# Moving the transposes of the next group by one step, and the exponentials of the taps by two, in a fused dynamic-convolution and gated-MLP kernel

## The chip, the cores and the metric

The kernel runs on one core of a Trainium2 chip. The metric is the device time of one execution in microseconds (us). The kernel before takes 1408.44 us, the median of 3 runs (1408.35 to 1408.87).

## The reference

Two parts follow each other. A dynamic convolution: for each of 4 x 4096 tokens and 8 heads, 7 tap weights go through a softmax and weigh the 7 last tokens. Then a gated MLP on the 16384 tokens, 192 wide inside and out, 1536 in the middle, all in float32:

```python
w = weight_gen - np.max(weight_gen, axis=-1, keepdims=True)
w = np.exp(w)
w = w / (np.sum(w, axis=-1, keepdims=True) + 1e-09)
out = np.einsum('bshk,bskhg->bshg', w, x_unf)
...
g = x @ w_gate
silu = g * (1.0 / (1.0 + np.exp(-g)))
val = x @ w_val
return (silu * val @ w_out).astype(np.float32)
```

## The kernel before, in words

**Tiling.** Each of 128 partitions holds 128 tokens. Tokens are taken in `NG` = 32 groups of 4 columns (`JG`), that is 512 tokens a group; the middle width of 1536 is taken in `NF` = 12 slices of 128. The program is a list of 384 steps (g, f), and step i is written out by the loop at L618. Values that need float32 precision are split in two float32r halves, hi and lo, so most products are three matmuls. Matmuls use 64 rows of the array at a time: one for `LOW` and one for `HIGH`, which run side by side.

**One step (g, f).** `up_first` (L432) makes 12 matmuls into two PSUM tiles `up` (gate and value); `up_second` (L445) makes the last 6. ScalarE (ACT) takes silu of the first tile into `sg` (L459); VectorE (DVE) multiplies `h` = value x `sg` (L473), ACT rounds it to `hi` (L474), DVE makes `lo` (L476). Two steps later (`LAG` = 2) `down` (L483, L503 and L512) multiplies them with `w_out` into four accumulators, in two pairs, each in two halves: four calls a step. In an ordinary step three of them stand between `up_first` and `up_second`, and one behind.

**The pool of PSUM tiles.** `ps_up` has 4 tiles in turn. A step takes 2; in a turn step the transposes take the other 2 (`tr`).

**The attention of the next group.** While group g is multiplied, DVE makes `xatt` of group g+1: 13 operations (7 products L230, 6 additions L260) that `spread` (L546) lays over the steps from f = 9 of group g-1 (`LEAD` = 3) to f = 5 of group g. After the last addition ACT copies the upper columns of `xatt` to their place (L263). Then comes the **turn step**, from the table `turned`: in steady groups f = 6. There 8 transposes (`turn`, L295, instructions at L299) stand behind `up_first`, `up_second` follows at once, all four calls of `down` come behind it, then 8 more transposes; then `split_ops` (L312) makes `xhi` (ACT, L317) and `xlo` (DVE, L324) for group g+1, which begins 5 steps later. An order between the two halves of a sum is kept by a marker on GpSimd's queue (`told`, L278: wait for one matmul; `behind`, L284: the other half waits for the marker).

**The softmax of the taps.** Taps come in 6 chunks of 12, 24, 24, 24, 24 and 20 columns (3 groups, then 6 groups each, 5 in the last). For each chunk c >= 2, between steps s0 and s1 (72 steps): 4 DVE operations before (max L169, subtract L176, in two pieces), one exponential on ACT (L182) at step `at`, 5/8 of the way, and behind it sums, reciprocals and normalisation on DVE (L187 to L199). Exp and silu use different function tables, so ACT loads a table before the exponential (L182) and one before the next silu (L459). `at` is step 66, 138, 210 and 282: f = 6 in groups 5, 11, 17 and 23, which is a turn step. Chunk 1 has a place of its own, `EXP1` = 16: group 1, f = 4.

**Start.** In group 0 the weights are still being converted by DVE, ACT and GpSimd (`weight_ops`), and the turn step is step 8 (`LEAD1` = 1).

Of the kernel before, what the change touches and what calls it, by code (L numbers as in the profile page):

```python
# [18 lines left out]
def dynconv_glu_kernel(  # L19
# [35 lines left out]
    NF = F // P  # L55
# [4 lines left out]
    EXP1 = 16  # L60
# [59 lines left out]
    def load_taps(c):  # L120

        j0, n = wcuts[c]
        wt = w_t[c] = soft.tile([P, NJ, H, K], F32, tag="wt", name="wt")
        pieces = {0: (0, JG, n), 1: range(0, n + 1, 2 * JG)}.get(c, (0, n))

        def load(a, b):
            nc.sync.dma_start(
                out=wt[:, a:b].rearrange("p t h k -> p t (h k)"), in_=wgr[:, j0 + a : j0 + b]
            )

        return [lambda a=a, b=b: load(a, b) for a, b in zip(pieces, pieces[1:])]

    def load_x(c):

        j0, n = xcuts[c]
        xt = x_t[c] = xin.tile([P, PAD + NX, D], F32, tag="xt", name="xt")
        pieces = {0: (0, JG, n), 1: range(0, n + 1, 2)}.get(c, (0, n))

        def load(a, b):
            own = PAD if c and a == 0 else 0  # L140
            nc.sync.dma_start(
                out=xt[:, PAD + a - own : PAD + b], in_=xr[:, j0 + a - own : j0 + b]
            )
            if c == 0 and a == 0:


                per = S // T
                for p0 in range(0, P, per):
                    nc.gpsimd.memset(xt[p0 : p0 + 1, 0:PAD], 0.0)
                    nc.sync.dma_start(  # L150
                        out=xt[p0 + 1 : p0 + per, 0:PAD],
                        in_=xr[p0 : p0 + per - 1, T - PAD : T],
                    )

        return [lambda a=a, b=b: load(a, b) for a, b in zip(pieces, pieces[1:])]
# [156 lines left out]
    def split_ops(g, ps):  # L312
        hi = [xts.tile([P, NC], F32R, tag=f"xhi{half}", name="xhi") for half in range(2)]

        def high(half):
            def go():
                nc.scalar.activation(out=hi[half], in_=ps[half], func=AF.Copy)  # L317

            return go

        def low(half):
            def go():
                lo = xts.tile([P, NC], F32R, tag=f"xlo{half}", name="xlo")
                nc.vector.tensor_tensor(  # L324
                    out=lo, in0=ps[half], in1=hi[half].bitcast(F32), op=ALU.subtract
                )
                xT[g, half] = hi[half], lo

            return go

        return [high(0), low(0), high(1), low(1)]
# [5 lines left out]
    def load_weights(f):  # L337
        raw = stage.tile([P, NW, 2], I32, tag="raw", name="raw", bufs=RAW)
        fs = slice(f * P, (f + 1) * P)
        pieces = (  # L340
            (raw[:, 0:P], w_gate[0:P, fs]),
            (raw[:, P : 2 * P], w_val[0:P, fs]),
            (raw[0:DB, 2 * P : 3 * P], w_gate[P:D, fs]),
            (raw[DB:P, 2 * P : 3 * P], w_val[P:D, fs]),
            (raw[:, 3 * P : NW], w_out[fs]),
        )
        for dst, src in pieces:
            nc.sync.dma_start(out=dst.rearrange("p n w -> p (n w)"), in_=src.bitcast(I32))
        raw_t[f] = raw
# [194 lines left out]
    turned = {}  # L544

    def spread(ops, first, last):  # L546

        for n, op in enumerate(ops):
            at = first + (n * (last - first)) // len(ops)
            todo.setdefault(max(at, 0), []).append(op)  # L550

    with tc.manual_schedule():
        nc.gpsimd.memset(exp_bias, -920.0 * TWO23)

        nc.scalar.activation(out=warm, in_=exp_bias, func=AF.Exp)
        now, soon = load_x(0)
        for op in load_taps(0) + [now]:
            op()
        load_weights(0)
        load_weights(1)  # L560
        soon()
        for f in range(2, RAW):
            load_weights(f)
        make_identity(nc, ident)

        before, exponentials, after = softmax_ops(0)
        for op in before:
            op()
        convert = [weight_ops(f) for f in range(NF)]
        w0, w1, w2, w3 = convert[:4]  # L570
        nc.scalar.activation(out=warm, in_=exp_bias, func=AF.Silu)
        asides, rest, joined = attention_ops(0)
        for op in after[:3] + asides + rest[:4] + w0[:1] + [joined] + rest[4:5]:
            op()
        for op in [w0[1], rest[5], w0[2], w1[0], w0[3]] + rest[6:]:
            op()
        turns = split_ops(0, turn_whole(0))
        for op in turns[0::2] + w1[1:4] + turns[1:2] + w2[:1] + turns[3:]:
            op()

        later = after[3:]
        loads = load_x(1) + load_taps(1)
        todo[0] = [w2[1], w3[0], w2[2]]
        for i in range(NF):
            ops = todo.setdefault(i, [])
            for f, part in ((i + 2, 3), (i + 3, 1), (i + 4, 0), (i + 3, 2)):
                if f < NF:
                    ops.append(convert[f][part])
        todo[0] += later[:3]
        spread(loads, LOAD1, LOAD1 + 7)  # L590
        spread(later[3:], NF - LEAD - 2, NF - LEAD)
        spread(
            [lambda f=f: split(wo[:, f, 0], wo[:, f, 1], wo32[:, f]) for f in range(NF)],
            WO,
            NF + LAG - 1,
        )
        for c in range(1, len(wcuts)):
            s0 = (wcuts[c - 1][0] // JG - 1) * NF - LEAD if c > 1 else NF
            s1 = (wcuts[c][0] // JG - 1) * NF - LEAD
            before, exponentials, after = softmax_ops(c)  # L600
            at = s0 + (s1 - s0) * 5 // 8 if c > 1 else EXP1
            if c + 1 < len(wcuts):
                todo.setdefault(s1, []).append(lambda c=c: load_taps(c + 1)[0]())
            spread(before, s0 + 1 - (c == 1), at)
            exps[at] = exponentials
            spread(after, at + 2, s1)
        for g in range(1, NG):
            s0 = (g - 1) * NF - (LEAD if g > 1 else LEAD1)
            c = first_x.get(g)
            if c and c + 1 < len(xcuts):  # L610
                todo.setdefault(s0, []).append(lambda c=c: load_x(c + 1)[0]())
            asides, rest, _ = attention_ops(g)
            spread(asides, max(s0, 0), s0 + NF - 4)
            spread(rest, max(s0, 0), s0 + NF - 3)
            turned[s0 + NF - 3] = g

        steps = [(g, f) for g in range(NG) for f in range(NF)]
        for i in range(len(steps) + LAG + 1):  # L618
            ops = todo.pop(i, [])
            to_turn = turned.get(i)  # L620
            if i < len(steps):
                g, f = steps[i]
                sums, nop = up_first(g, f)
                if i in exps:
                    exps[i]()
            late = []
            if i > LAG:
                late = [(*steps[i - LAG - 1], 1, True)]
            if i > LAG and not to_turn:
                down(*late.pop())  # L630
            if to_turn:
                ps = [ps_up.tile([P, NC], F32, tag="up", name="tr") for _ in range(2)]
                turned_nop = turn(to_turn, ps, None)
            if LAG <= i < len(steps) + LAG:
                s = steps[i - LAG]
                late += [(*s, 0, False), (*s, 1, False), (*s, 0, True)]
                if not to_turn:
                    down(*late.pop(0))
                    if s[1]:
                        down(*late.pop(0))  # L640
                    else:
                        late.reverse()
            if i < len(steps):
                up_second(g, f, sums, nop)
                sg = silu(sums)
            for what in late:
                down(*what)
            if i > LAG:
                h_t.pop(steps[i - LAG - 1])
            if to_turn:  # L650
                turn(to_turn, ps, turned_nop)
            if i < len(steps):

                def between():
                    if ops:
                        ops.pop(0)()
                    return ops

                gated(g, f, sums, sg, between)
            if to_turn:  # L660
                for op in split_ops(to_turn, ps):
                    op()
            for op in ops:
                op()
# [33 lines left out]
```

## Time and profile before

| what | value |
|---|---|
| median of 3 runs | 1408.44 us |
| the profiled execution, its own time | 1409.2 us |
| its span, first to last instruction | 1407.4 us |
| PE (TensorE matmul) busy | 1300.9 us, 92% |
| PEld (TensorE weight load) busy | 1220.4 us, 87% |
| DVE (VectorE) busy | 1010.4 us, 72% |
| ACT (ScalarE) busy | 610.2 us, 43% |
| POOL (GpSimd) busy | 71.8 us, 5% |
| granted TensorE clock, mean | 0.988 |
| chain that ended last | PE 83%, DVE 8%, ACT 4%, DMA 2% |

Busy time is the union of an engine's instructions. PE counts matmuls whose ends are modelled, and LOW and HIGH matmuls overlap, so an instruction's length is more than the spacing of two. A row of the timeline gives start and length in us; "[0.76 <-X]" is idle time of that engine just before, and what ended it. A wait for several semaphores is put down to the one that the profile saw last. PEclk is the share of full clock that was granted to TensorE.

### The profile page before, as it was taken

How to read it: one execution, taken by the hardware profiler on the slowest of the kernel's cores; microseconds unless marked ns; L12 is line 12 of the kernel's file. 1: busy time of each engine (PE TensorE's matmuls, PEld its weight loads, DVE VectorE, ACT ScalarE, POOL GpSimd, SP SyncE). 2: the span in 40 equal slices, each digit the busy share in tenths (PEclk: the TensorE clock that was granted, in tenths of full speed). 3: DMA queues.
4: the chain of work that ended last, by engine and by line, in shares of the span. 5: the costliest groups of instructions: out<-in, count | busy, mean ns of one | idle time of the engine just before them, and what ended most of it. 6: DMA issues, size and time to landing. Idle time of an engine off the chain costs nothing.

```text
span 1407.4 us, 31625 instructions
## 1 busy us (share of the span) xinstructions
PE 1300.9 (92%) x13560; PEld 1220.4 (87%) x13560; DVE 1010.4 (72%) x1385; ACT 610.2 (43%) x1073; POOL 71.8 (5%) x66
## 2 busy tenths in 40 slices
PE   0479999999999999999999999999999999999998
PEld 0359899989999998999999899989989899999998
DVE  2997867768777777877777777777777776677743
ACT  1445444454444445444344544444454444444443
POOL 3673000000000000000000000000000000000000
PEclk9989999999999999999999999999999999999999
DMA  3341010101001010100101001010100101000000
GB/s 96 97 156 32 13 41 13 52 13 51 13 21 52 13 52 12 51 13 21 52 13 52 13 22 43 18 51 13 52 13 13 41 13 52 13 13 13 13 13 13
DMA packets 28460, 47.36 MB, mean 34 GB/s; under 512 B 1956, under 2 KB 25508, under 8 KB 26528
## 3 DMA queue, kind: packets, MB, share of 16 engines
q1 hardware_dynamic: 28320, 45.34, 9.7%
q8 instruction: 106, 1.74, 0.5%
q14 instruction: 34, 0.28, 0.1%
HBM read 32.75 MB, written 12.58 MB: 32 GB/s over the span
## 4 chain that ended last, share of the span: by engine, by line
PE 83%; DVE 8%; ACT 4%; DMA 2%; issue 1%; SPq 0%; ACTq 0%; DVEq 0%
PE dn L503 22%; PE up L451 19%; PE up L439 18%; PE up L442 17%; PE dn L512 6%; DVE xatt L260 3%; DVE h L473 2%; DMA xt<-in_x_dram 2%; ACT sg L459 2%; PE tr L299 1%; ACT xatt L263 1%; DVE m L389 1%; DVE w L402 1%; DVE m L379 0%; PE dn L496 0%
## 5 line engine op out<-in xcount | busy, mean ns | idle before, releaser
L503 PE MATMUL dn<-wo,hi 64*128 64x384 f32 x2976 | 612.7, 347 | 0.4 <-ACT hi L474 0.4
L512 PE MATMUL dn<-wo,lo 64*128 64x192 f32 x2976 | 543.0, 249 | 0.3 <-DVE lo L476 0.3
L503 PEld LDWEIGHTS dn<-wo,hi 64*128 64x128 f32 x2976 | 480.0, 185 | 14.9 <-ACT hi L474 0.6
L473 DVE TENSOR_TENSOR h<-up,sg 128x512 f32<-128x512 f32 x372 | 257.1, 691 | 289.5 <-ACT sg L459 289.4
L512 PEld LDWEIGHTS dn<-wo,lo 64*128 64x128 f32 x2976 | 444.8, 187 | 9.6 <-DVE lo L476 0.5
L459 ACT ACTIVATE sg<-up 128x512 f32<-128x512 f32 x384 | 229.7, 598 | 435.7 <-PE up L451 405.0
L474 ACT ACTIVATE hi<-h 128x512 fp32r<-128x512 f32 x372 | 235.2, 632 | 294.7 <-DVE h L473 294.7
L476 DVE TENSOR_TENSOR lo<-h,hi 128x512 fp32r<-128x512 f32 x372 | 255.8, 688 | 70.5 <-ACT hi L474 70.5
L439 PE MATMUL up<-xhi,wb_hi 64*128 64x512 f32 x768 | 246.8, 425 | 10.8 <-ACT sg L459 7.5
L451 PE MATMUL up<-xhi,wa_hi 64*128 64x512 f32 x768 | 240.4, 427 | 9.8 <-POOLq L280 9.7
L439 PE MATMUL up<-xlo,wb_hi 64*128 64x512 f32 x768 | 234.0, 395 | 0.9 <-DVE xlo L324 0.9
L439 PE MATMUL up<-xhi,wb_lo 64*128 64x512 f32 x768 | 234.0, 396 | 0.0
L442 PE MATMUL up<-xhi,wa_lo 64*128 64x512 f32 x768 | 233.0, 393 | 0.0
L442 PE MATMUL up<-xhi,wa_hi 64*128 64x512 f32 x768 | 233.0, 393 | 0.0
L442 PE MATMUL up<-xlo,wa_hi 64*128 64x512 f32 x768 | 231.8, 390 | 0.0
L451 PE MATMUL up<-xhi,wa_lo 64*128 64x512 f32 x768 | 226.1, 392 | 0.0
L451 PE MATMUL up<-xlo,wa_hi 64*128 64x512 f32 x768 | 225.6, 391 | 0.0
L230 DVE TENSOR_TENSOR prod<-xt,wt 128x768 f32<-128x768 f32 x186 | 182.0, 979 | 0.1
L260 DVE TENSOR_TENSOR xatt<-xatt,prod 128x768 f32<-128x768 f32 x186 | 180.7, 971 | 0.0
L439 PEld LDWEIGHTS up<-xhi,wb_hi 64*128 64x128 f32 x768 | 138.3, 186 | 16.4 <-ACT sg L459 8.3
L442 PEld LDWEIGHTS up<-xlo,wa_hi 64*128 64x128 f32 x768 | 138.9, 187 | 8.1
L442 PEld LDWEIGHTS up<-xhi,wa_lo 64*128 64x128 f32 x768 | 138.1, 185 | 8.8
(57 smaller groups left out, 1370.3 us busy)
## 6 DMA issues: line engine op xcount, KB each, us to landing
xt<-in_x_dram SPq DMA_DIRECT2D x14, 1344.0 KB, 5.6
out_dram<-osb SPq DMA_DIRECT2D x31, 384.0 KB, 2.6
raw<-in_moe_w_out_dram SPq DMA_DIRECT2D x12, 192.0 KB, 2.7
wt<-in_weight_gen_dram SPq DMA_DIRECT2D x3, 672.0 KB, 3.9
raw<-in_moe_w_gate_dram SPq DMA_DIRECT2D x12, 128.0 KB, 2.6
raw<-in_moe_w_val_dram SPq DMA_DIRECT2D x12, 128.0 KB, 2.6
wt<-in_weight_gen_dram SPq DMA_DIRECT2D x4, 224.0 KB, 3.7
xt<-in_x_dram SPq DMA_DIRECT2D x2, 384.0 KB, 3.7
```

Of the source, the lines that this page charges most:

```text
L230: engine.tensor_tensor(out=into.rearrange("p t (h i) -> p t h i", h=H), in0=src, in1=w, op=ALU.mult)
L260: nc.vector.tensor_tensor(out=a, in0=a, in1=tmp.pop(k), op=ALU.add)
L263: nc.scalar.activation(out=a[:, :, D:], in_=a[:, :, P:D], func=AF.Copy)
L439: nc.tensor.matmul(ps, w[r, fs], m[r], start=(n == 0), stop=False)
L442: ins = nc.tensor.matmul(sums[i], w[r, i, fs], m[r], start=False, stop=False)
L451: ins = nc.tensor.matmul(sums[i], w[r, i, fs], m[r], start=False, stop=(n == len(full) - 1))
L459: nc.scalar.activation(out=sg, in_=sums[0], func=AF.Silu)
L473: nc.vector.tensor_tensor(out=h, in0=sums[1], in1=sg, op=ALU.mult)
L474: nc.scalar.activation(out=hi, in_=h, func=AF.Copy)
L476: nc.vector.tensor_tensor(out=lo, in0=h, in1=hi.bitcast(F32), op=ALU.subtract)
L503: nc.tensor.matmul(acc[t], hi[r, cs], wo[r, f].rearrange("p a d -> p (a d)"), start=opens, stop=False,)
L512: nc.tensor.matmul(acc[t][:, 0:D], lo[r, cs], wo[r, f, 0], start=False, stop=closes)
```

## The change

Two numbers in the schedule. `at` becomes 2 steps earlier for chunks 2 to 5 (steps 64, 136, 208, 280: f = 4), and with it the DVE operations that are spread before and behind it move by 0 to 2 steps. `turned` becomes one step later for every group (f = 7; in group 0 step 9).

```diff
-            at = s0 + (s1 - s0) * 5 // 8 if c > 1 else EXP1
+            at = s0 + (s1 - s0) * 5 // 8 - 2 if c > 1 else EXP1
             if c + 1 < len(wcuts):
                 todo.setdefault(s1, []).append(lambda c=c: load_taps(c + 1)[0]())
             spread(before, s0 + 1 - (c == 1), at)
             exps[at] = exponentials
             spread(after, at + 2, s1)
...
             spread(rest, max(s0, 0), s0 + NF - 3)
-            turned[s0 + NF - 3] = g
+            turned[s0 + NF - 2] = g
```

TensorE's queue in group 1, the step f = 6, before (`dn_...` are accumulators; order gives the output's shape). The transposes stand directly behind `up_first`:

```order
L442 MATMUL up<-xhi,wa_lo 128x512 x2
L299 MATMUL tr<-ident,xatt 128x64 x8
L451 MATMUL up<-xhi,wa_hi 128x512 x2
L451 MATMUL up<-xlo,wa_hi 128x512 x2
L451 MATMUL up<-xhi,wa_lo 128x512 x2
L503 MATMUL dn_1064<-wo,hi 128x384
```

The same queue with the change, the end of `up_first` of f = 7 and what follows:

```order
L442 MATMUL up<-xhi,wa_lo 128x512 x2
L299 MATMUL tr<-ident,xatt 128x64 x8
L451 MATMUL up<-xhi,wa_hi 128x512 x2
L451 MATMUL up<-xlo,wa_hi 128x512 x2
L451 MATMUL up<-xhi,wa_lo 128x512 x2
L503 MATMUL dn_1065<-wo,hi 128x384
```

The neighbours are the same; one whole step of f = 6 in its ordinary order, with three calls of `down` ahead of `up_second`, now stands ahead of them.

ScalarE's queue in group 5, before: the exponentials stand behind the copy of `xatt` (L263) and ahead of the silu of the turn step, whose split (L317) follows.

```order
L459 ACTIVATE sg<-up 128x512
L474 ACTIVATE hi<-h 128x512
L263 ACTIVATE xatt<-xatt 128x4x64
L182 ACT_TABLE_LOAD
L182 ACTIVATE wt<-wt 128x1344
L459 ACT_TABLE_LOAD
L459 ACTIVATE sg<-up 128x512
L474 ACTIVATE hi<-h 128x512
L317 ACTIVATE xhi<-tr 128x512 x2
```

With the change they stand two steps ahead of the copy, and three ahead of the turn step's silu:

```order
L182 ACT_TABLE_LOAD
L182 ACTIVATE wt<-wt 128x1344
L459 ACT_TABLE_LOAD
L459 ACTIVATE sg<-up 128x512
L474 ACTIVATE hi<-h 128x512
L459 ACTIVATE sg<-up 128x512
L474 ACTIVATE hi<-h 128x512
L263 ACTIVATE xatt<-xatt 128x4x64
L459 ACTIVATE sg<-up 128x512
L474 ACTIVATE hi<-h 128x512
L459 ACTIVATE sg<-up 128x512
L474 ACTIVATE hi<-h 128x512
```

No instruction is added or removed on any engine; no load or store moves.

## Rows read from the trace of the kernel before

**Rows 1.** The page, part 1: busy time, share of the span and instructions of each engine.

```profile
PE 1300.9 (92%) x13560; PEld 1220.4 (87%) x13560; DVE 1010.4 (72%) x1385; ACT 610.2 (43%) x1073; POOL 71.8 (5%) x66
```

**Rows 2.** The waits of PE: engine, line, waited for: us in total, times, longest.

```profile
PE tr L299 <- DVE xatt L260: 27.7, 31, 4.3
...
PE up L439 <- ACT sg L459: 7.5, 4, 1.9
```

**Rows 3.** Timeline, PE, a turn step of group 13: start, length (us), what, [idle before <-releaser].

```profile
637.77 0.57 PE L442 MATMUL up<-xhi,wa_lo 64*128 64x512 f32 x2
639.10 0.76 PE L299 MATMUL tr<-ident,xatt 64*128 64x64 f32 x7 [0.76 <-DVE xatt L260]
639.67 0.48 PE L451 MATMUL up<-xhi,wa_hi 64*128 64x512 f32 x1
...
641.69 0.41 PE L299 MATMUL tr<-ident,xatt 64*128 64x64 f32 x8
641.90 0.74 PE L439 MATMUL up<-xhi,wb_hi 64*128 64x512 f32 x2
```

**Rows 4.** Timeline, PEld, the same step: the first weight load of the transposes.

```profile
639.07 0.14 PEld L299 LDWEIGHTS tr<-ident,xatt 64*128 64x128 f32 x1 [1.16 <-ACT hi L474]
```

**Rows 5.** Timeline, ACT, the same step: sg of f=5, f=6 and f=7, and hi of f=5.

```profile
636.77 0.60 ACT L459 ACTIVATE sg<-up 128x512 f32<-128x512 f32 x1 [1.22 <-PE up L451]
638.12 0.63 ACT L474 ACTIVATE hi<-h 128x512 fp32r<-128x512 f32 x1 [0.76 <-DVE h L473]
...
640.76 0.60 ACT L459 ACTIVATE sg<-up 128x512 f32<-128x512 f32 x1 [1.36 <-PE up L451]
...
645.45 0.60 ACT L459 ACTIVATE sg<-up 128x512 f32<-128x512 f32 x1 [1.73 <-PE up L451]
```

**Rows 6.** Timeline, DVE, the same step: h, the last add into xatt, the next h.

```profile
637.40 0.69 DVE L473 TENSOR_TENSOR h<-up,sg 128x512 f32<-128x512 f32 x1 [0.26 <-ACT sg L459]
638.01 0.95 DVE L260 TENSOR_TENSOR xatt<-xatt,prod 128x768 f32<-128x768 f32 x1
...
641.39 0.69 DVE L473 TENSOR_TENSOR h<-up,sg 128x512 f32<-128x512 f32 x1 [1.83 <-ACT sg L459]
```

**Rows 7.** Timeline, ACT, the turn step with the exponentials of chunk 2 (group 5).

```profile
300.59 0.60 ACT L459 ACTIVATE sg<-up 128x512 f32<-128x512 f32 x1 [1.23 <-PE up L451]
...
303.80 0.60 ACT L459 ACTIVATE sg<-up 128x512 f32<-128x512 f32 x1 [1.22 <-PE up L451]
...
306.46 1.28 ACT L182 ACT_TABLE_LOAD   x1
307.75 1.33 ACT L182 ACTIVATE wt<-wt 128x1344 f32<-128x1344 f32 x1
...
310.39 0.60 ACT L459 ACTIVATE sg<-up 128x512 f32<-128x512 f32 x1
...
316.66 0.60 ACT L459 ACTIVATE sg<-up 128x512 f32<-128x512 f32 x1 [3.31 <-PE up L451]
```

**Rows 8.** Windows behind the four exponentials: us, busy by engine, PEclk, DMA share, GB/s.

```profile
313.10:316.40 3.30, 3.30 (x25) 3.17 (x22) 1.20 (x3) 0.25 (x1) 0.00 (x0) 0.50 0.02 5
...
559.00:562.00 3.00, 1.90 (x13) 1.38 (x15) 1.45 (x3) 2.23 (x5) 0.00 (x0) 1.00 0.00 0
809.00:811.20 2.20, 2.20 (x16) 1.92 (x14) 1.46 (x3) 0.51 (x2) 0.00 (x0) 0.50 0.00 0
1057.20:1060.40 3.20, 3.20 (x23) 2.92 (x20) 1.89 (x3) 0.96 (x2) 0.00 (x0) 0.50 0.00 0
```

**Rows 9.** Timeline, PE, around the exponentials of chunk 1 (group 1, f=4 to 6).

```profile
136.97 0.39 PE L442 MATMUL up<-xhi,wa_lo 64*128 64x512 f32 x2
...
140.99 0.39 PE L442 MATMUL up<-xhi,wa_lo 64*128 64x512 f32 x1
...
141.22 0.39 PE L442 MATMUL up<-xhi,wa_lo 64*128 64x512 f32 x1
142.99 0.76 PE L299 MATMUL tr<-ident,xatt 64*128 64x64 f32 x7 [1.37 <-DVE xatt L260]
```

## The prediction

> **What bounds the kernel now.** I read the page first: TensorE is busy for 92% of the span, twice as long as ScalarE and well above VectorE [rows 1]. So time can come only out of TensorE's idle stretches, or out of stretches at a lower clock. The view of waits comes next. Once the start is over, TensorE waits in two places worth naming: before the transposes (27.7 us in 31 waits, one for each turn step) and, four times, in `up_first` for a silu (7.5 us, longest 1.9) [rows 2]. These are the places of the two edits. Then the timeline of one turn step of each kind, on every engine, because a wait's total does not tell what else shifts when it ends earlier.
>
> An ordinary turn step. `up_first` ends at 637.77 + 0.57 = 638.34, the transposes start at 639.10 after 0.76 idle, `up_second` at 639.67 [rows 3]. On VectorE, h of the step before ends at 637.40 + 0.69 = 638.09, but the last addition into `xatt` only at 638.01 + 0.95 = 638.96 [rows 6]. The first weight load of the transposes follows 0.11 us behind that, at 639.07 [rows 4]. So the turn step comes one addition too early: what it reads is finished 0.87 us after the PSUM tile that it needs is free. From silu to silu the two steps around it take 645.45 - 636.77 = 8.68 us [rows 5], against 2 x 3.21 for ordinary steps (303.80 - 300.59 = 3.21) [rows 7]. A turn costs 2.26 us.
>
> A turn step with exponentials. ScalarE does table load, exponentials and table load from 306.46 to 310.39, 3.93 us, before it reaches the silu of that very step [rows 7]. In a turn step all four PSUM tiles are in use, so the next `up_first` needs this silu and the h behind it, and TensorE stands still. Silu to silu takes 310.39 - 303.80 = 6.59 and then 316.66 - 310.39 = 6.27 us [rows 7], in place of 3.99 and 4.69 [rows 5]: 2.60 and 1.58 more. The second part is clock: behind three of the four stalls TensorE ran with a granted clock of 0.50 (1.2 GHz), behind the second one at 1.00 [rows 8]; before each fall it had stood idle. The four cost 4 x 2.60 + 3 x 1.58 = 15.1 us.
>
> **The change, part by part.** Nothing is added or removed and no DMA moves; GpSimd's and SyncE's queues stay as they are.
>
> Turn one step later. The last addition stays in f = 5, so at f = 7 `xatt` and its copy have been complete for a whole step. What the transposes then wait for is the PSUM tile, whose reader h ended at 638.09 in the phase of the group shown. With the same 0.11 us to the weight load they start at 638.20; eight of them take 641.90 - 641.69 = 0.21 us when nothing holds them [rows 3], which is 638.41. `up_second` also needs the marker behind `up_first`, whose last matmul ends at 638.34; with a hop through GpSimd, taken at 0.16 us (a little over the 0.11 of one hop), it starts at 638.50 in place of 639.67. That is 1.17 us. Everything behind it in the step (silu, h, four calls of `down`, the second transposes, the next `up_first` that waits for h) hangs on that start by fixed lengths, so all of it shifts. Bounds: 0.76, the idle that the profile shows [rows 3], and 1.26, which would leave 1.00 of the 2.26. 29 steady turn steps (groups 2 to 30): 29 x 1.17 = **33.9 us** (22.0 to 36.5).
>
> What the later split asks: `xhi` and `xlo` are first read 4 steps later in place of 5, so nothing there comes late. Eight turn steps now get one softmax operation of VectorE into them (f = 7 of steps 43, 79 and so on, in chunks 2 to 5). I cost these at nothing, because VectorE idles 1.83 us before the turn step's h [rows 6]; were that cover gone, each would cost at most about the 0.95 of an addition [rows 6], 7.6 us in all.
>
> Exponentials at f = 4. No row shows chunks 2 to 5 there, but chunk 1 has stood at f = 4 all along, with the same number of columns, so its rows are the nearest. One step after them the last matmuls of `up_first` start at 140.99 and 141.22 [rows 9]; a step earlier they started at 136.97, so without a wait they were due at 136.97 + 3.21 = 140.18. TensorE lost 0.81 to 1.04 us there, and stood still far less than in a turn step, because in an ordinary step two of the four tiles are spare and a silu may be a step late. I take 0.9 each. 15.1 - 4 x 0.9 = **11.5 us** (7.5, if each still costs the 1.9 of [rows 2], to 15.1, if none costs anything).
>
> ScalarE: Activation LUTs of the Trainium skill, section What ACT_TABLE_LOAD costs, states a drain of 1.38 us behind each load of 1.28, 2.66 for a switch. Here the exponentials start at 307.75, right where the load of 306.46 + 1.28 ends [rows 7], so the trace disagrees. By the page, two drains would add 2.76 us to each late silu, the four would cost about 4 x 3.7, and this term would be 0.3 in place of 11.5 (an estimate by that page).
>
> Group 1. Its turn step waited 1.37 us [rows 9], 0.61 more than an ordinary one, because chunk 1's exponentials are two steps ahead of it; now they are three ahead. 1.17 + 0.61 = **1.8 us** (0.6 to 2.0).
>
> Group 0. The turn step waited 4.3 us, the longest wait of the 31, for an addition that VectorE reached late between weight conversions [rows 2]. With the turn put off, the second half of that step can run in the hole, but the next `up_first` then waits for h, which VectorE makes right behind that addition. Between 0 and 4.3 I take the middle, **2.1 us**.
>
> **The sum.** 33.9 + 11.5 + 1.8 + 2.1 = 49.3 us. The profiled execution took 1409.2 us, 0.76 more than the median of the runs: 1409.2 - 49.3 = 1359.9, and 1359.1 against the median. Ends: 22.0 + 7.5 + 0.6 + 0 - 7.6 = 22.5 to 36.5 + 15.1 + 2.0 + 4.3 = 57.9, so 1350.5 to 1385.9. The lower gains would have to meet all at once.
>
> **The rivals.**
>
> *The transposes are released by something else.* The profile puts their first weight load down to `hi` on ScalarE [rows 4], not to the addition. Were that the true releaser, of the step just before, delaying the step would leave most of the wait. hi ends at 638.12 + 0.63 = 638.75 [rows 5]; start at 638.86, `up_second` near 639.17, gain 0.5 each: 14.5 + 11.5 + 1.1 + 2.1 = 29.2, that is 1379.2. For it: the row's name. Against it: the load comes 0.11 us behind the addition's end and 0.3 behind hi, and the transposes read nothing that hi writes.
>
> *The stall moves with the exponentials.* Then the second term is about nothing, and 37.8 us are left: 1370.6. Were only the clock to fall as before, three times 1.58 us would be kept: 1364. For it: nothing is shortened on ScalarE. Against it: chunk 1's rows [rows 9]. The page TensorE: Matmul & The Clock Gate of the Trainium skill (HAM oscillation) says that waits between bursts bring the clock down again and again; rows 8 agree for stalls of the old size.
>
> *Slower: the turn step's own h comes late.* In a turn step the next `up_first` waits for h of the same step, so each microsecond by which VectorE is late there is paid in full, 29 times. VectorE had 1.83 us to spare; silu comes 1.17 earlier, and 0.66 stays. Were VectorE still busy with a backlog at that point, the whole is slower only from 1.17 + 15.4/29 = 1.7 us of lateness on, 2.36 us of backlog: two and a half additions. With three, 2.85 us, each turn would lose 2.19 - 1.17 = 1.02 us net, 29.6 against 15.4 from the other terms: 1422.6. Against it: between f = 5 and f = 7 no attention is left to do, so there is nothing for a backlog to be made of.
>
> **How the numbers follow.** The forecast, 1359.1, has 0.76; the first rival 0.08; the second 0.12, in either size; slower 0.02; and 0.02 for a new wait that eats the gain exactly. The range of 1351 to 1374 reaches from the best end over the second rival and leaves the first rival and the other signs out. A measurement of this kernel can tell about 0.2%, 2.8 us, from no change. Faster by more 0.96, within 0.02, slower 0.02.
>
> **What would show it.** Right: the wait of L299 for `xatt` is gone but for a few tenths each; the two silu gaps around an ordinary turn add up to about 7.5 us in place of 8.68; behind the exponentials the wait for silu or h is below 1 us, and no window at half clock stands at the four places. Wrong: L299 still waits over 0.4 us a time, with hi or h named as its releaser; TensorE idles over 1.5 us at f = 4 to 6 of groups 5, 11, 17 and 23; or a new wait of `up_first` for `xlo` or h in turn steps.

## The result, and the profile after

The change takes 1360.97 us (median of 4 runs, 1360.93 to 1361.69) against 1408.65 us for the kernel before: a ratio of 0.9662, 95% interval 0.9645 to 0.9679. The forecast was 1359.1 us, with a range of 1351 to 1374. The profiled execution took 1360.93 us, 48.3 less than that of before; the forecast for this difference was 49.3.

From the page after: the span, busy times, and the granted clock in tenths over 40 slices.

```profile
span 1359.1 us, 31623 instructions
...
PE 1286.0 (95%) x13560; PEld 1204.6 (89%) x13560; DVE 1009.7 (74%) x1385; ACT 608.6 (45%) x1073; POOL 71.8 (5%) x66
...
PEclk9989999999999999999999999999999999999999
```

TensorE is busy for 95% of a shorter span, where [rows 1] had 92%. Its own busy time falls by 14.9 us too; part of that are the stretches at half clock behind the exponentials [rows 8], which are gone (a window below).

The waits of PE after (engine, line, waited for: us in total, times, longest):

```profile
PE up L451 <- POOLq L280: 10.6, 7, 3.1
...
PE tr L299 <- DVE h L473: 1.8, 4, 0.5
PE tr L299 <- DVE hi L468: 1.3, 1, 1.3
PE up L439 <- DVE h L473: 1.2, 5, 0.2
```

Both waits of [rows 2] are gone: of 27.7 us before the transposes 3.1 are left (1.8 in four waits for h, and one of 1.3 in group 0), of 7.5 us for a silu nothing. The five short waits of `up_first` for h, 1.2 us in all, were there before, behind the waits for the silu and in group 1 (1.1 us).

The turn step of group 13, now f = 7, as [rows 3] on PE: the end of `up_first`, the transposes, `up_second`, the second transposes.

```profile
620.33 0.57 PE L442 MATMUL up<-xhi,wa_lo 64*128 64x512 f32 x2
620.57 0.58 PE L299 MATMUL tr<-ident,xatt 64*128 64x64 f32 x8
621.01 0.50 PE L451 MATMUL up<-xhi,wa_hi 64*128 64x512 f32 x2
...
623.01 0.40 PE L299 MATMUL tr<-ident,xatt 64*128 64x64 f32 x8
```

There is no idle time ahead of the transposes at 620.57 any more: the first of them follows the last matmuls of `up_first` directly. The weight loads show what held the others. Of the first eight transposes the later seven stand in one row on PEld, here before and then after the change:

```profile
639.46 0.32 PEld L299 LDWEIGHTS tr<-ident,xatt 64*128 64x128 f32 x7 [0.25 <-ACT xatt L263]
```

```profile
620.69 0.32 PEld L299 LDWEIGHTS tr<-ident,xatt 64*128 64x128 f32 x7 [0.22 <-DVE h L473]
```

Before, they waited for the copy of the upper columns of `xatt` on ScalarE, which comes behind the addition and ends at 639.41. After, they wait for h of f = 6, the reader of the PSUM tile (on VectorE from 619.95 to 620.64), and no longer for `xatt`. `up_second` starts 0.37 us behind the end of h; the forecast had 0.41. On ACT, as [rows 5], the silu and hi of f = 6 and the silus of f = 7 and 8:

```profile
619.32 0.60 ACT L459 ACTIVATE sg<-up 128x512 f32<-128x512 f32 x1 [0.57 <-PE up L451]
620.67 0.63 ACT L474 ACTIVATE hi<-h 128x512 fp32r<-128x512 f32 x1 [0.76 <-DVE h L473]
622.08 0.60 ACT L459 ACTIVATE sg<-up 128x512 f32<-128x512 f32 x1 [0.78 <-PE up L451]
...
626.77 0.60 ACT L459 ACTIVATE sg<-up 128x512 f32<-128x512 f32 x1 [1.73 <-PE up L451]
```

The two steps around the turn take 626.77 - 619.32 = 7.45 us, where [rows 5] had 8.68. All of the gain is in the first of them, 2.76 in place of 3.99; the second keeps its 4.69. The table gives the length of whole groups, from the silu (L459) of f = 0 to that of the next group's f = 0:

| groups | before | after | difference |
|---|---|---|---|
| 0 | 65.65 | 63.88 | 1.77 |
| 1 | 43.26 | 41.49 | 1.77 |
| the 21 others, 2 to 30 | 40.74 to 40.80 | 39.50 to 39.58 | 1.24 on average |
| 4, 10, 16, 22 | 40.74 to 40.80 | 40.13 to 40.18 | 0.61 to 0.64 |
| 5, 11, 17, 23 (exponentials) | 44.97, 43.37, 44.94, 44.78 | 40.51, 40.50, 40.52, 40.30 | 4.46, 2.87, 4.42, 4.48 |

Two rows need a look. Groups 5, 11, 17 and 23 are still 0.97, 0.96, 0.98 and 0.76 us longer than ordinary ones (the last has the chunk of 20 columns, the others 24). Group 5 on ACT (the silu of f = 3, the exponentials, the silus of f = 4 and 5), the idle time of PE behind it, and a window (us, busy by engine, PEclk, DMA share, GB/s):

```profile
290.85 0.60 ACT L459 ACTIVATE sg<-up 128x512 f32<-128x512 f32 x1 [0.62 <-PE up L451]
...
292.86 1.28 ACT L182 ACT_TABLE_LOAD   x1
294.15 1.33 ACT L182 ACTIVATE wt<-wt 128x1344 f32<-128x1344 f32 x1
...
296.79 0.60 ACT L459 ACTIVATE sg<-up 128x512 f32<-128x512 f32 x1
...
298.69 0.58 ACT L459 ACTIVATE sg<-up 128x512 f32<-128x512 f32 x1
```

```profile
298.17 0.50 PE L439 MATMUL up<-xhi,wb_hi 64*128 64x512 f32 x1 [0.24 <-DVE h L473]
```

```profile
296.00:302.00 6.00, 5.76 (x58) 4.84 (x56) 4.23 (x6) 4.05 (x7) 0.00 (x0) 1.00 0.00 0
```

The silu of f = 4 comes 5.94 us after that of f = 3, 2.73 late; TensorE still has 0.24 us of plain idle time and a first pair of matmuls that goes one at a time, and the clock stays at 1.00, as it does behind the other three.

And groups 4, 10, 16 and 22 gain only half. Group 4, ACT (hi of f = 5, the copy of `xatt`, the silu of f = 6), DVE (the subtraction of the softmax and the last addition into `xatt`, both in f = 5), and PE (the rest of the first transposes):

```profile
258.45 0.63 ACT L474 ACTIVATE hi<-h 128x512 fp32r<-128x512 f32 x1 [0.76 <-DVE h L473]
260.71 0.42 ACT L263 ACTIVATE xatt<-xatt 128x256 f32<-128x256 f32 x1 [1.63 <-DVE xatt L260]
261.03 0.58 ACT L459 ACTIVATE sg<-up 128x512 f32<-128x512 f32 x1
```

```profile
258.33 0.85 DVE L176 TENSOR_TENSOR wt<-wt,mx 128x672 f32<-128x672 f32 x1
...
259.73 0.95 DVE L260 TENSOR_TENSOR xatt<-xatt,prod 128x768 f32<-128x768 f32 x1
```

```profile
262.39 0.40 PE L299 MATMUL tr<-ident,xatt 64*128 64x64 f32 x6 [0.45 <-DVE h L473]
```

The forecast did not have this. The move of the exponentials also moves the four softmax operations that are spread ahead of them, and the last one (L176) lands in f = 5. It is issued between h and lo, so the addition, which usually stands there, comes behind lo and ends at 259.73 + 0.95 = 260.68. The copy waits 1.63 us for it at the head of ScalarE's queue, and the silu of f = 6, whose input is ready, starts only behind the copy. So h of f = 6 is late, and the transposes of f = 7 wait 0.45 us for it.

### The profile page after: what moved, and what is told of

It is laid out like the page before. It is cut to its first block, busy times and chain, and to the rows that moved or that the text cites. A ratio compares the mean times of both kernels' runs of the same rounds, so it can differ in the third digit from the quotient of the medians.

```text
span 1359.1 us, 31623 instructions
## 1 busy us (share of the span) xinstructions
PE 1286.0 (95%) x13560; PEld 1204.6 (89%) x13560; DVE 1009.7 (74%) x1385; ACT 608.6 (45%) x1073; POOL 71.8 (5%) x66
## 4 chain that ended last, share of the span: by engine, by line
PE 87%; DVE 6%; ACT 3%; DMA 2%; issue 1%; SPq 0%; POOL 0%; ACTq 0%; DVEq 0%; POOLq 0%
PE dn L503 21%; PE up L439 20%; PE up L451 20%; PE up L442 18%; PE dn L512 5%; DMA xt<-in_x_dram 2%; PE tr L299 1%; DVE h L473 1%; DVE xatt L260 1%; ACT sg L459 1%; DVE w L402 1%; DVE m L389 1%; ACT wt L182 0%; ACT L459 0%; DVE hi L468 0%
## 5 line engine op out<-in xcount | busy, mean ns | idle before, releaser
L503 PE MATMUL dn<-wo,hi 64*128 64x384 f32 x2976 | 598.5, 346 | 0.4 <-ACT hi L474 0.4
L512 PE MATMUL dn<-wo,lo 64*128 64x192 f32 x2976 | 530.3, 248 | 0.3 <-DVE lo L476 0.3
L459 ACT ACTIVATE sg<-up 128x512 f32<-128x512 f32 x384 | 229.4, 597 | 380.7 <-PE up L451 346.4
L439 PE MATMUL up<-xhi,wb_hi 64*128 64x512 f32 x768 | 242.7, 425 | 4.8 <-DVE hi L468 2.8
L451 PE MATMUL up<-xhi,wa_hi 64*128 64x512 f32 x768 | 233.4, 425 | 10.7 <-POOLq L280 10.6
L439 PE MATMUL up<-xlo,wb_hi 64*128 64x512 f32 x768 | 229.5, 395 | 0.9 <-DVE xlo L324 0.9
L439 PE MATMUL up<-xhi,wb_lo 64*128 64x512 f32 x768 | 229.2, 395 | 0.0
L442 PE MATMUL up<-xhi,wa_hi 64*128 64x512 f32 x768 | 227.8, 392 | 0.0
L442 PE MATMUL up<-xhi,wa_lo 64*128 64x512 f32 x768 | 227.5, 392 | 0.0
L442 PE MATMUL up<-xlo,wa_hi 64*128 64x512 f32 x768 | 226.6, 389 | 0.0
L451 PE MATMUL up<-xhi,wa_lo 64*128 64x512 f32 x768 | 219.8, 391 | 0.0
L451 PE MATMUL up<-xlo,wa_hi 64*128 64x512 f32 x768 | 219.0, 389 | 0.0
L439 PEld LDWEIGHTS up<-xhi,wb_hi 64*128 64x128 f32 x768 | 137.4, 185 | 11.2 <-DVE hi L468 3.8
L442 PEld LDWEIGHTS up<-xhi,wa_hi 64*128 64x128 f32 x768 | 137.3, 186 | 9.3
```

Of the source, the lines that this page charges most:

```text
L439: nc.tensor.matmul(ps, w[r, fs], m[r], start=(n == 0), stop=False)
L442: ins = nc.tensor.matmul(sums[i], w[r, i, fs], m[r], start=False, stop=False)
L451: ins = nc.tensor.matmul(sums[i], w[r, i, fs], m[r], start=False, stop=(n == len(full) - 1))
L459: nc.scalar.activation(out=sg, in_=sums[0], func=AF.Silu)
L503: nc.tensor.matmul(acc[t], hi[r, cs], wo[r, f].rearrange("p a d -> p (a d)"), start=opens, stop=False,)
L512: nc.tensor.matmul(acc[t][:, 0:D], lo[r, cs], wo[r, f, 0], start=False, stop=closes)
```

## The experiments

My theory after the result: (1) a turn gains because `xatt` is complete, not because f = 7 is a better step; (2) the stall at the exponentials is dear where PSUM tiles are short, that is on the turn step and just ahead of it (the runs below move the exponentials and the turn; none changes the number of tiles, so the tiles as the reason are read from the program and the waits); (3) the lost half in groups 4, 10, 16 and 22 comes from the copy that blocks ScalarE. The rivals stand in the expectations. All ratios are to runs of the kernel before on the same chip, whose medians there were 1408.99 (first four), 1409.26 (next three) and 1410.44 us (last two).

### The turn alone

```diff
-            turned[s0 + NF - 3] = g
+            turned[s0 + NF - 2] = g
```

> The transposes one step later (f = 7), the exponentials left at f = 6. My theory: each turn gains 1.25 us by itself (29 times, with 1.8 each in groups 0 and 1: 39.9 us), and the exponentials gain nothing, because the transposes at f = 7 take the PSUM tiles of step f = 6 and wait for its late silu and h: still about 2.7 us of stall at each of the four, perhaps with a stretch at half clock behind it. Total 1368 to 1371 us. Rival, by which the stall belongs to the turn step alone: the four stalls shrink to about 1 us each as soon as the turn step is another one, about 1358.

1372.7 us, ratio 0.9740 (0.9726 to 0.9755): the theory, 1.7 us over its range. All ordinary groups take 39.54 us, 4, 10, 16 and 22 among them, since no softmax operation is in f = 5 here. Groups 5, 11, 17 and 23 take 45.22, 42.88, 44.12 and 43.86, so the exponentials cost 5.7, 3.3, 4.6 and 4.3 us over an ordinary group, more than before the change (4.2, 2.6, 4.2 and 4.0). The waits of PE, two windows in group 5 and one in group 11 (us, busy by engine, PEclk, DMA share, GB/s):

```profile
PE tr L299 <- ACT sg L459: 9.6, 4, 2.4
```

```profile
299.00:303.00 4.00, 1.92 (x18) 1.48 (x15) 0.00 (x0) 3.96 (x4) 0.00 (x0) 1.00 0.00 0
303.00:309.80 6.80, 6.08 (x45) 5.90 (x47) 3.24 (x5) 3.25 (x6) 0.00 (x0) 0.52 0.01 2
546.00:553.00 7.00, 6.26 (x73) 5.77 (x75) 3.96 (x6) 3.06 (x6) 0.00 (x0) 1.00 0.01 2
```

The stall has changed its place and become longer: in these four groups the transposes wait up to 2.4 us for the silu of f = 6, where `up_first` had waited 1.9, and behind it in group 5 the clock is 0.52 for 6.8 us. Group 11 waits as long, keeps the full clock, and costs least of the four. A step next to the turn is no better than the turn itself.

### The exponentials alone

```diff
-            at = s0 + (s1 - s0) * 5 // 8 if c > 1 else EXP1
+            at = s0 + (s1 - s0) * 5 // 8 - 2 if c > 1 else EXP1
```

> The exponentials at f = 4, the transposes left at f = 6. My theory: the four stalls shrink from 15.1 us in all to about 1.5 each (as chunk 1, two steps ahead of a turn), 9 us gained; but the subtraction of the softmax that the edit brings into f = 5 puts the last addition into xatt off by 1.4 us in groups 4, 10, 16 and 22, and before a turn at f = 6 that is paid in full: 5.6 us lost. Total about 1405. Rival, by which the moved VectorE operations are hidden: about 1399.5. If the parts of the change just add, it must be 1408.65 less what the first edit alone leaves of the 47.7 us.

1410.67 us, ratio 1.0013 (1.0004 to 1.0023): no gain at all. The waits of PE before the transposes, PE in group 5, and a window behind it:

```profile
PE tr L299 <- DVE xatt L260: 35.7, 31, 4.3
```

```profile
305.83 0.50 PE L439 MATMUL up<-xhi,wb_hi 64*128 64x512 f32 x1 [0.22 <-DVE h L473]
...
308.86 0.76 PE L299 MATMUL tr<-ident,xatt 64*128 64x64 f32 x7 [1.37 <-DVE xatt L260]
```

```profile
309.80:313.00 3.20, 3.20 (x25) 3.20 (x25) 1.18 (x2) 1.05 (x2) 0.00 (x0) 0.51 0.00 0
```

The part on the subtraction came out: groups 4, 10, 16 and 22 take 42.14 to 42.19 us, 1.38 more than their neighbours (5.5 in all, 5.6 expected), and the wait for `xatt` grows from 27.7 to 35.7 us. What I missed is the clock. The stall at f = 4 is small as forecast (0.22 idle), but the delayed turn two steps on idles 1.37 more, and behind the pair TensorE's granted clock is 0.51; there was such a stretch in each of the four groups, which take 43.40 to 43.62 us, 2.6 to 2.9 more than an ordinary one in place of 1.5. Four times 1.3 us more is the difference to the 1405 that I expected. That it is the clock's price is read from the trace: a fall cost 1.58 us before [rows 7], and in the run above group 17, with a fall, took 1.24 more than group 11, without one.

So the two edits don't add. Alone they give -36.3 and +1.7 us, together -47.7: 13 us of the gain exist only when both are made.

### The attention one step earlier

The kernel before, with the turn and the exponentials left in place:

```diff
-            spread(rest, max(s0, 0), s0 + NF - 3)
+            spread(rest, max(s0, 0), s0 + NF - 4)
```

> The kernel before, with the attention operations of the next group spread over 8 steps in place of 9, so that the last addition stands in f = 4, and the transposes and the exponentials where they were (f = 6). My theory: the gain of the turn is that xatt is complete, not the place of the step, so each turn gains the same 1.25 us, and the wait of L299 for xatt is gone: about 1370, with the four exponential stalls as before. Rival, by which f = 7 itself is the better place: no gain, 1408, or a loss, since VectorE now has four steps with two attention operations in eight.

1388.22 us, ratio 0.9849 (0.9834 to 0.9863), 18 over the 1370 expected. The theory holds where nothing else is in the way: ordinary groups take 39.53 us, as with the change, with the turn still at f = 6. But groups 6, 7, 12, 13, 18, 19, 24 and 25 stay at 40.78 to 40.91. Group 6 on ACT and DVE:

```profile
344.61 0.42 ACT L263 ACTIVATE xatt<-xatt 128x256 f32<-128x256 f32 x1 [1.63 <-DVE xatt L260]
344.93 0.58 ACT L459 ACTIVATE sg<-up 128x512 f32<-128x512 f32 x1
```

```profile
342.23 0.85 DVE L199 TENSOR_TENSOR wt<-wt,sm 128x672 f32<-128x672 f32 x1
...
343.62 0.95 DVE L260 TENSOR_TENSOR xatt<-xatt,prod 128x768 f32<-128x768 f32 x1
```

It is the mechanism of group 4 again: a normalisation (L199) falls into f = 4, where the last addition now is, the addition ends at 344.57, and the copy holds up the silu. The exponential groups take 43.80 to 45.39 us, and the waits of PE show why:

```profile
PE up L439 <- ACT sg L459: 10.5, 5, 2.5
...
PE tr L299 <- DVE h L473: 4.1, 9, 0.5
```

Five waits for a silu, 10.5 us in all and up to 2.5 long, where [rows 2] had four, 7.5 and 1.9: what the turn step no longer waits for `xatt`, it waits for the silu. 8 x 1.29 and 22 in place of 15 us for the exponentials make up 17 of the 18; group 1, which takes 43.69 us where about 42 was expected, lost another 1.7 (it has the fifth wait).

### The copy behind the silu

The changed kernel; the copy leaves `add` and is issued in f = 6 (only the first group's copy, ahead of the steps, stays where it was):

```diff
-                    nc.scalar.activation(out=a[:, :, D:], in_=a[:, :, P:D], func=AF.Copy)
...
                 sg = silu(sums)
+                if i + 1 in turned:
+                    copy_of(turned[i + 1])
```

> The changed kernel, with the copy of xatt on ScalarE (L263) issued one step later, right behind the silu of f = 6. My theory: in groups 4, 10, 16 and 22 the copy stands at the head of ScalarE's queue and holds back the silu of f = 6 until the late addition is done, which costs 0.63 us each; with the copy behind that silu the four 0.63 us are gone: 1358.5, 2.5 us less than the change, and silu to silu 3.22 and 2.76 in these groups as in the others. Rival, by which VectorE itself makes h late there: no difference, 1361.

1359.29 us, ratio 0.9645 (0.9631 to 0.9659). The total alone doesn't tell it from the change, whose interval overlaps, and group 0 took 1.2 us longer in this profile (it takes 63.5 to 65.1 in the kernels that turn at step 9 or later). The groups do: 4, 10, 16 and 22 take 39.55, 39.57, 39.55 and 39.55, like all others, and the 0.63 us are gone. Group 4 on ACT (lines are 3 higher in this kernel; the copy is L222):

```profile
261.08 0.60 ACT L462 ACTIVATE sg<-up 128x512 f32<-128x512 f32 x1 [1.23 <-PE up L454]
261.57 0.41 ACT L222 ACTIVATE xatt<-xatt 128x256 f32<-128x256 f32 x1
262.43 0.63 ACT L477 ACTIVATE hi<-h 128x512 fp32r<-128x512 f32 x1 [0.45 <-DVE h L476]
```

The silu comes first, the copy fits between silu and hi, and the addition is as late as before without harm. VectorE's lateness is not the cause; the queue behind the copy is.

### The turn at f = 8

```diff
-            turned[s0 + NF - 2] = g
+            turned[s0 + NF - 1] = g
```

> The changed kernel with the transposes one more step later (f = 8). My theory: after one step xatt is complete, so a second step gives nothing in ordinary groups; only the four times 0.63 us of groups 4, 10, 16 and 22 go, because the late silu of f = 6 then has a spare step: about 1358.5. Rival, by which putting the turn off pays for every step: another 1.2 us a turn, below 1330.

1357.52 us, ratio 0.9629 (0.9613 to 0.9645). Ordinary groups stay at 39.5 us: the second step gives nothing there. Groups 4, 10, 16 and 22 take 39.52 to 39.55, although the silu of f = 6 is 0.7 us late as in the change; the next step makes it up before the transposes ask for it.

### The exponentials on the turn step again

```diff
-            at = s0 + (s1 - s0) * 5 // 8 - 2 if c > 1 else EXP1
+            at = s0 + (s1 - s0) * 5 // 8 + 1 if c > 1 else EXP1
```

> The changed kernel with the exponentials put on the turn step again, now f = 7. My theory: in a turn step all four PSUM tiles are taken, so the late silu is paid in full: 2.6 us each, and 1.6 more where the clock falls behind the idle time, in place of 0.97; and the subtraction is no longer in f = 5, which gives back 2.5 us. About 1361 + 4 x 3.2 - 2.5 = 1371, between 1366 (no fall of the clock) and 1374. Rival, by which f = 6 was the bad place: 1358 to 1361.

1380.3 us, ratio 0.9791 (0.9777 to 0.9806): the direction of the theory, 6 us beyond its upper end. The waits of PE, and a window behind the stall of group 5:

```profile
PE up L439 <- ACT sg L459: 9.8, 4, 2.5
PE tr L299 <- DVE h L473: 3.6, 8, 0.5
```

```profile
308.20:311.20 3.00, 3.00 (x19) 2.55 (x17) 1.89 (x3) 1.16 (x3) 0.00 (x0) 0.50 0.03 5
```

Four waits of up to 2.5 us for the silu, each with half clock behind it, cost 4.4 to 5.9 us in place of the 4.2 I took from f = 6. The rest, about 5 us, is the copy once more: eight groups (6, 7, 12, 13 and so on) take 40.2 us, because the normalisation now falls into f = 5. These are the eight waits for h. In group 6 the copy again waits 1.63 us for the addition, ahead of the silu; no run moves the copy here, so this part is read from the trace.

### The exponentials at f = 5

With the later copy, so that this alone differs from it:

```diff
-            at = s0 + (s1 - s0) * 5 // 8 - 2 if c > 1 else EXP1
+            at = s0 + (s1 - s0) * 5 // 8 - 1 if c > 1 else EXP1
```

> The changed kernel with the later copy of the run before (L263 behind the silu of f = 6) and the exponentials at f = 5, two steps ahead of the turn in place of three. My theory: the silu of f = 6 is still about 1.5 us late then, and the transposes at f = 7 need its h at once, so each of the four costs about 0.8 us more: 1361.5. Rival, by which only the turn step itself is dear: no difference to the later copy alone, 1358.5.

1361.1 us, ratio 0.9655 (0.9641 to 0.9669). Groups 5, 11, 17 and 23 take 40.98 to 41.13 us against 40.34 to 40.50 with f = 4: 0.6 more each, where 0.8 was expected. Two steps ahead of the turn are nearly enough, three are better.

### Both remedies, and no exponentials

First the later turn and the later copy together (the copy leaves `add` as before):

```diff
-            turned[s0 + NF - 2] = g
+            turned[s0 + NF - 1] = g
...
                 sg = silu(sums)
+                if i + 2 in turned:
+                    copy_of(turned[i + 2])
```

> The transposes at f = 8 and the copy of xatt behind the silu of f = 6, together. My theory: both take away the same loss, the late silu of f = 6 in groups 4, 10, 16 and 22, so together they give what the better one gives alone: about 1357.5. Rival, by which they are two different gains: about 1355.

1357.41 us, ratio 0.9629 (0.9615 to 0.9642), the same as the turn at f = 8 alone: one loss, removed twice. These two are the fastest versions of this study, about 3.5 us under the change; the interval of the turn at f = 8 just touches that of the change, the other's ends at 0.9642, below its 0.9645. Of the 3.5, the group lengths bear out 2.5, the four groups.

And the changed kernel without the exponentials of chunks 2 to 5:

```diff
-            exps[at] = exponentials
+            if c == 1:
+                exps[at] = exponentials
```

> The changed kernel without the exponentials of chunks 2 to 5 and without their eight table loads (the taps of these chunks are weighed without the exponential). My theory: what is left of the four stalls at f = 4 is 0.97, 0.97, 0.97 and 0.76 us, and ScalarE's 3.9 us are otherwise hidden: about 1357.3, and groups 5, 11, 17 and 23 as long as the others, 39.5 us. Rival, by which the remaining excess of these groups comes from the VectorE operations of the softmax: no change, 1361.

1357.89 us, ratio 0.9633 (0.9620 to 0.9647). Groups 5, 11, 17 and 23 take 39.53 to 39.56 us, like all others, so the 3.7 us left at f = 4 belong to the exponentials with their table loads and to nothing else. Groups 4, 10, 16 and 22 keep their 40.16 to 40.18: the subtraction is still in f = 5.

## Why the prediction was right, point by point

- **The turn.** Forecast 1.17 us each, from the earlier start of `up_second`. Measured 1.24 in ordinary groups, near the upper bound of 1.26. The attention drawn forward gives the same 39.53 us with the turn at f = 6, so the reason was the right one: `xatt` was not complete. One reading was short: the prediction looked at the first weight load alone and held the step to come "one addition too early", by 0.87 us. The other seven loads stood until the copy behind the addition ended at 639.41, 1.32 us after the tile was free. The sum did not suffer, since it went by the start of `up_second`, which has both in it.
- **The exponentials.** Forecast 15.1 - 4 x 0.9. Measured in group lengths 14.9 - 3.7 = 11.2 us against 11.5. Chunk 1 in [rows 9] was a good stand-in (chunk 5 has 20 columns, not "the same number", and left 0.76). But the forecast put this down as a term of its own, and it isn't one: with the turn left at f = 6 the same move gained nothing.
- **Groups 1 and 0.** Forecast 1.8 and 2.1, measured 1.77 and 1.77. For group 0 the middle between 0 and 4.3 was taken, so that it fits is luck; and group 0 differs by over a microsecond between profiles of kernels that are alike there, so its size is not settled.
- **The step that failed** is the cost of the moved softmax operations. "I cost these at nothing" was said of f = 7, and there it holds. The one that counts went into f = 5, which the forecast did not look at, and it cost 4 x 0.63 = 2.5 us by way of ScalarE's queue. With it the sum is 29 x 1.24 + 11.2 + 1.8 + 1.8 - 2.5 = 48.3, the difference of the two profiles, as it must be, since these are the lengths of the groups. That the forecast came within 1.0 us of it is in part luck: the turn gave 2.1 us more than its 33.9, and the missed operations took 2.5.
- **The rivals.** `hi` as the releaser of the transposes fell: at f = 7 the first starts at 620.57 and the loads of the others at 620.69, while hi of f = 6 runs from 620.67 to 621.30. The stall that moves with the exponentials did not happen at f = 4, but it is real: at f = 6 with the turn at f = 7 it was 2.4 us of waiting each. The late h of the turn step turned up in the four groups, at 0.45 us of idle time, far from the 1.7 that would decide. ScalarE: Activation LUTs of the Trainium skill, section What ACT_TABLE_LOAD costs, states a drain for each switch of tables. It doesn't show after the change either: the exponentials start at 294.15, 1.29 us behind the start of the load of 1.28.

## What to carry to other kernels

When a step waits for a product of another engine, ask first whether its place is one operation too early; here one step of delay took all of that wait in ordinary groups, and a second took nothing more there. An operation that waits on an in-order queue costs what stands behind it, so a copy that may come late belongs behind the work that is ready. Moving one entry of a spread table moves all that is spread up to it: look up where each piece lands, and on whose queue the next one then waits.

## What the runs showed of the hardware that I had not expected

The same idle time does not always bring the clock down. With the exponentials alone, 0.22 and then 1.37 us of idle time were followed by about 3 us at 0.51 in group 5. Group 1 of the kernel before has the same pair behind chunk 1's exponentials ([rows 9]: 1.37 before the transposes), and a window over it, of the kernel before, shows the full clock:

```profile
139.00:145.00 6.00, 4.23 (x40) 3.03 (x38) 4.23 (x6) 2.69 (x6) 0.00 (x0) 1.00 0.24 98
```

Nor did the second of the four stalls before the change cost any clock ([rows 8], 559 to 562), while 2.44 us in the turn alone were followed by 6.8 us at 0.52 in group 5, and by the full clock in group 11 of the same run. So the prediction's "rows 8 agree" is true of three stalls out of four. A schedule that leaves stalls of 1.4 us or more in this program paid for them now at full clock and now with half clock behind them. What decides between the two I can't say from these rows.
